# Sigmoid attention and a gated MLP on one core: SyncE's transfers in program order, the small sums as a step of their own, Q's part between two sigmoids

## The chip, the core and the metric

The kernel runs on one core of a Trainium2 chip. The core has five engines with a queue of instructions each: TensorE (PE, matrix products into PSUM; PEld is its loading of weights), VectorE (DVE), ScalarE (ACT), GpSimd (POOL), and SyncE (SP), which here only issues transfers. Each engine works through its queue in order and waits on semaphores for the others. The metric is the device time of one execution in microseconds (us), less is better.

## The reference

Eight batches of twelve heads, 448 tokens of 64 numbers each. Attention weighs with a sigmoid instead of a softmax; the heads are laid side by side into rows of 768, and an MLP follows whose gate is h - tanh(h).

```python
# q, k, v: (8, 12, 448, 64)   w_in: (768, 2048)   w_out: (2048, 768)
scores = q @ k.transpose(0, 1, 3, 2) / sqrt(64) - log(448)
x = (1 / (1 + exp(-scores))) @ v          # then (8 * 448, 768)
h = x @ w_in
out = (h - tanh(h)) @ w_out
```

Everything is float32 outside. Inside, a number is mostly split into two float16 parts, scaled by a power of two, and a product is made of three matmuls (high by high, high by low, low by high).

## The kernel before, in words

**Batches.** Batch 0 is computed in float32 (`attention32`, `moe1_32`), while both weight matrices are loaded, converted and split. From then on each batch b does two things: `moe1` (L748), the product with `w_in` with the gate computed by `mix` behind it, and `moe2` (L857), the product with `w_out`. The attention of batch b + 1 runs in small steps between the matmuls of `moe2` of batch b. Batch 1 keeps its attention weights in float32 (`AV32 = 2`); batches 2 to 7 split them.

**Positions.** `moe2` is a generator: it gives way after every six full-width matmuls (`po`, L876), 48 times, and then 16 times after six half-width ones (`por`, L914), which count half. A table (`BLOCKS`; `BLOCKS0` and `BLOCKS1` for batches 0 and 1) holds the positions at which the next step of the attention is taken from the generator `stream` (L451). So the order of each engine's queue is written out by hand.

**Steps.** `stream` goes by pairs of heads (g, h = g + 1), four steps each, which this document calls A to D. `sc` are scores in PSUM (L380), `a` their sigmoid on ACT (L391), `ahl` the two float16 parts of `a` (high on ACT L397, rest on DVE L398), `acc` the product of `ahl` with the parts `vhl` of v (L411), `x` the evacuated `acc` (L425 or L427).

- A: scores and sigmoids of g's row blocks 0 and 1; the products `acc` left over from the steps before; `ahl`; square sums of v (`sqn`, L317).
- B: scores and sigmoids of g's block 2 and of the half block that g and h share; square sums of k and q of head g + 3; `ahl`.
- C: `scales(g + 2)`, which is a tiny matmul `pbn` (L325) over the square sums, its evacuation `tn` on ACT (L327), and a chain of six tiny DVE instructions to the scales `sn` (L336); scores of h's blocks 0 and 1; its first sigmoid; K's part of head g + 2; its second sigmoid; the products `acc`; `vhl`; `ahl`; Q's part of g + 2; loads of head g + 4.
- D: scores and sigmoid of h's block 2; K's part, `ahl`, Q's part of head g + 3; square sums of head g + 4.

A "part" (`parts`, L345) turns a loaded k or q into two float16 halves `w` (first half L351 on ACT or L353 on DVE, second half L354 on DVE) and then transposes them by a DMA that SP issues (L356) into the tile K or Q, which the scores read. `w` has two buffers.

**Queues.** The whole program stands in a block that keeps PE, ACT, DVE and POOL in the order in which the code is written. SP isn't named there: its transfers are put in an order by the framework's scheduler.

**Square sums of x.** `add_squares` (L431) sums the squares of the six `x` tiles of a batch: two of the six squares are made on ACT (L437), the other four on POOL (L439), all sums on POOL (L448).

**Weights in batch 0.** While `moe2` of batch 0 runs, the pieces of `w_out` (`rawo`, L131, then `stb` on ACT L146 and DVE L151 to L155, and a small matmul `wl`, L179) are still converted, and `w_in` and `w_out` (`wi`, `wo`) are split on ACT (L216) and DVE (L219), at positions of their own between the steps.

Of the kernel before, what the change touches and what calls it, by code (L numbers as in the profile page):

```python
# [34 lines left out]
class Builder:  # L35
# [4 lines left out]
    SPLIT = 16, 0.78  # L40
    CONV = 0.95

    BLOCKS = (8, 11, 16, 20, 24, 27, 32, 36, 40, 43, 48, 52)
    TAIL = (1, 2, 3, 4, 5)
    ALONE = 9
    BLOCKS0 = (2, 5, 8, 12, 16, 20, 24, 31, 38)
    BLOCKS1 = (4, 7, 10, 13, 16, 20, 24, 27, 32, 36, 40, 43, 48, 52)

    TP = 8
    SHIFT = 4  # L50
# [368 lines left out]
    def evac_x(self, j, acc, iv):  # L419
        nc = self.nc  # L420
        x = self.xp.tile([P, self.S], F32, name="x32", tag="x")
        if iv is None and self.xs is None:
            nc.vector.tensor_copy(x, acc[:, : self.S])  # L423
        elif iv is None:
            nc.scalar.activation(x, acc[:, : self.S], AF.Copy)  # L425
        else:
            nc.scalar.activation(x, acc[:, : self.S], AF.Copy, scale=iv)  # L427
        self.add_squares(j, x)
        return x

    def add_squares(self, j, x):  # L431

        nc = self.nc
        last = j == self.NP - 1
        x2 = self.xp.tile([P, self.S], BF16 if last else F32, name="x2", tag="x2", bufs=2)
        if last or j == 0:
            nc.scalar.activation(x2, x, AF.Square)  # L437
        else:
            nc.gpsimd.tensor_tensor(x2, x, x, op=ALU.mult)  # L439
        if j == 0:  # L440
            self.x2 = x2
        elif last:
            self.x2b = self.x2, x2
        else:
            out = self.x2
            if j == self.NP - 2:
                out = self.xp.tile([P, self.S], BF16, name="x2b", tag="x2b", bufs=1)
            nc.gpsimd.tensor_tensor(out, self.x2, x2, op=ALU.add)  # L448
            self.x2 = out

    def stream(self):  # L451

        NP = self.NP
        G = (self.B - 1) * NP
        at = lambda g: (1 + g // NP, g % NP)
        splits = lambda g: at(g)[0] >= self.AV32
        qk, vn, sc, K, Q, vv, accs = {}, {}, {}, {}, {}, {}, {}  # L460

        def load(g):
            if g < G and g not in qk:
                qk[g] = self.load_qk(*at(g))

        def load_v(g):
            if g < G and splits(g):
                vn[g] = self.load_v(*at(g), self.nat, "vn", 2)

        def sums(g):  # L470
            ss = self.sums[g // 2 % 2]
            return ss if splits(g) else ss[:, :4]

        def norms(g):
            if g < G:
                for n, t in enumerate(qk[g]):
                    self.norm(t, sums(g)[:, 2 * n + g % 2 : 2 * n + g % 2 + 1])

        def norm_v(g):
            if g in vn:  # L480
                self.norm(vn[g], sums(g)[:, 4 + g % 2 : 5 + g % 2])

        def scales(g, where):
            if g < G:
                sc[g] = sc[g + 1] = self.scales(sums(g), where)

        def parts_k(g):
            if g < G:
                K[g] = self.parts(qk[g][0], sc[g][0][:, 0:1], "K", not splits(g) and g not in (2, 3))

        def parts_q(g):
            if g < G:
                Q[g] = self.parts(qk[g][1], sc[g][0][:, 1:2], "Q", True)
                qk.pop(g)

        def prep_v(g):
            if g >= G:
                return
            if splits(g):
                vv[g] = self.prep_v(vn.pop(g), sc[g][0])  # L500
            else:
                vv[g] = self.load_v(*at(g), self.att, "vhl", 3)[:, None]

        load(0)
        load(1)
        yield 0, False
        norms(0)
        norms(1)
        yield 0, False
        scales(0, "tr")  # L510
        parts_k(0)
        yield 450, False
        parts_q(0)
        load(2)
        yield 450, False
        parts_k(1)
        yield 450, False
        parts_q(1)
        load(3)
        yield 450, False  # L520
        norms(2)
        yield 0, False
        todo = []

        def open_acc(g):
            tag = "tr" if g % 2 else "av"
            accs[g] = self.ps.tile([P, 512], F32, name="acc", tag=tag, bufs=1)
            if g % NP == 0:
                self.xs = []

        def close_acc(g):
            iv = sc[g][1][:, 1:2] if splits(g) else None
            self.xs.append(self.evac_x(g % NP, accs.pop(g), iv))
            if g % 2:
                vv.pop(g - 1)
                vv.pop(g)
            for d in (sc, K, Q):
                d.pop(g)

        def do_av():  # L540
            for g, c, A in todo:
                odd = g % 2
                if c == QT:
                    open_acc(g + 1)
                    self.av([accs[g], accs[g + 1]], vv[g], A, c, odd)
                    close_acc(g)
                    continue
                if c == 0 and not odd:
                    open_acc(g)
                self.av([accs[g]], vv[g], A, c, odd)  # L550
                if c == QT - 1 and odd:
                    close_acc(g)
            todo.clear()

        def units(g, cs, between=lambda: None):

            pss = []
            for c in cs:
                n = 2 if c == QT else 1
                pss.append(self.scores([K[g + i] for i in range(n)], [Q[g + i] for i in range(n)], c))  # L560
            aa = [self.weigh(pss[0], sc[g][1][:, 0:1])]
            between()
            aa += [self.weigh(ps, sc[g][1][:, 0:1]) for ps in pss[1:]]
            return aa

        def keep(g, cs, aa):
            if splits(g):
                aa = [self.split_a(a) for a in aa]
            todo.extend((g, c, a) for c, a in zip(cs, aa))

        for g in range(0, G, 2):
            h = g + 1
            early = g == 0

            aa = units(g, (0, 1))
            do_av()
            if early:
                prep_v(0)
                prep_v(1)
            keep(g, (0, 1), aa)  # L580
            load(g + 3)
            norm_v(g + 2)
            norm_v(g + 3)
            yield 2750, True

            aa = units(g, (2, QT))
            if early:
                do_av()
            norms(g + 3)
            keep(g, (2, QT), aa)  # L590
            yield 2750, True

            scales(g + 2, "mm" if early else "av")
            aa = units(h, (0, 1), lambda: parts_k(g + 2))
            do_av()
            prep_v(g + 2)
            keep(h, (0, 1), aa)
            parts_q(g + 2)
            prep_v(g + 3)
            load(g + 4)  # L600
            load_v(g + 4)
            load_v(g + 5)
            yield 2750, True

            aa = units(h, (2,), lambda: parts_k(g + 3))
            if early:
                do_av()
            keep(h, (2,), aa)
            parts_q(g + 3)
            norms(g + 4)  # L610
            yield 2750, True
        do_av()
        yield 1150, True
# [314 lines left out]
    def build(self):  # L928
        nc, tc = self.nc, self.tc
# [19 lines left out]
        E = mybir.EngineType  # L949
        with tc.manual_schedule(engines={E.PE, E.Activation, E.DVE, E.Pool}):  # L950
# [5 lines left out]
            self.blocks = self.stream()  # L956
            self.moe1_32(self.xs, weights, rest)
            self.first(self.convert([(q, False) for q in pieces[nA + self.NF :]]))
            for b in range(1, self.B):
                self.batch(b)  # L960
        self.gp.release()

    def first(self, rest):

        n = 4
        next(self.tail)
        ahead = [self.split_w_out(0)]
        for k in range(n):
            next(self.blocks)
            for _ in range(2):  # L970
                next(self.tail, None)
            if k == 1:
                next(ahead[0])
            if k == 2:
                self.finish_g()
                next(ahead[0])
# [1 line left out]
        next(rest)  # L978
        next(ahead[0])
        next(rest)  # L980
        assert n + len(self.BLOCKS0) + len(self.BLOCKS1) == 4 * self.NP + len(self.BLOCKS) - self.ALONE
        split = self.split_w_in()
        at, each = self.SPLIT
        events = [(at + k * each, lambda: next(split, None)) for k in range(self.NC * self.NB + 1)]
# [7 lines left out]
            ahead[0] = self.split_w_out(1)  # L992

        events += [(at, scale)] + [(at + 0.5 * k, lambda: next(ahead[0], None)) for k in range(1, self.NF // 2 + 1)]
        self.second(0, self.BLOCKS0, 2 * self.NP - n, events)

    def batch(self, b):

# [69 lines left out]
```

## Time and profile before

| what | value |
| --- | --- |
| runs shown | 1250.58 us median of 3 (1249.23 to 1251.46) |
| the profiled execution, its own time | 1250.92 us |
| its span, first to last instruction | 1249.1 us |
| mean granted clock of PE | 0.982 |
| q1 (SP's transfers) | 88.28 MB, 31.1% of 16 DMA engines' span |

A row of the timeline gives the start in us, the duration in us, the engine, the line in the kernel, the operation with its tiles (written `out<-in`), the shape, how many in a row, and in brackets how long the engine stood idle before it and what released it. A row of the waits gives the waiting engine and tile, what it waited for, the total in us, how often, and the longest. A row of the table by stretches gives, for each engine, the busy time and the number of instructions, then PE's granted clock as a share of full speed, the busy share of the DMA engines, and GB/s.

### The profile page before, as it was taken

What the parts mean: (1) busy time and instruction counts of PE and PEld (TensorE: products, weight loads), DVE (VectorE), ACT (ScalarE), POOL (GpSimd) and SP (SyncE); (2) the same over time, 40 slices, a digit from 0 to 9 for tenths busy, and PEclk for the clock granted to TensorE, in tenths of its full rate; (3) what the DMA queues carried; (4) which work ended last, traced back from release to release, by engine and by line L of the source; (5) the groups of instructions that cost most, each with busy time, mean ns of one, the idle gap of its engine ahead of it and who ended that gap; (6) DMA issues with size and microseconds to landing.
All of it is one profiled execution on the core that took longest, in us unless ns stands there. A gap on an engine that the chain in (4) does not pass through costs nothing.

```text
span 1249.1 us, 19741 instructions
## 1 busy us (share of the span) xinstructions
PE 1183.5 (95%) x7633; PEld 612.2 (49%) x7633; DVE 932.9 (75%) x1376; ACT 884.6 (71%) x1230; POOL 87.3 (7%) x70
## 2 busy tenths in 40 slices
PE   8889976699989999999999999999999999999998
PEld 3235423255545555555555555545555555555555
DVE  5889977867975789767985789757985789736930
ACT  5657775865887768776888768776888768754820
POOL 0200001000002000110001000110001000110000
PEclk9899979799999999999999999999999999999999
DMA  9973448230034420253014420354014420310000
GB/s 227 257 209 83 90 89 216 57 87 14 1 73 101 87 51 1 66 113 89 1 30 100 87 52 1 70 116 82 1 30 100 87 52 1 58 29 20 1 13 33
DMA packets 225679, 89.78 MB, mean 72 GB/s; under 512 B 213936, under 2 KB 215728, under 8 KB 225584
## 3 DMA queue, kind: packets, MB, share of 16 engines
q1 hardware_dynamic: 224656, 88.28, 31.1%
q8 instruction: 60, 0.98, 0.3%
q10 hardware_dynamic: 928, 0.23, 0.1%
q14 instruction: 35, 0.29, 0.1%
HBM read 58.20 MB, written 11.01 MB: 55 GB/s over the span
## 4 chain that ended last, share of the span: by engine, by line
PE 65%; DVE 13%; ACT 10%; issue 6%; DMA 5%; SPq 1%; DVEq 0%; ACTq 0%
PE ph L761 30%; PE po L876 17%; PE acc L411 6%; PE por L914 5%; PE sc L380 5%; DMA Q<-w 3%; DVE ahl L398 3%; ACT ahl L397 3%; ACT a L391 2%; ACT sqn L317 2%; DVE sta L152 1%; DMA rawo<-moe_w_out 1%; DVE w L354 1%; DVE m L835 1%; DVE m L846 1%
## 5 line engine op out<-in xcount | busy, mean ns | idle before, releaser
L876 PE MATMUL po<-wo,g 128*128 128x384 f16 x2304 | 393.4, 327 | 4.6 <-DVE wo L219 2.0
L761 PE MATMUL ph<-xhl,wi 128*128 128x448 f16 x2016 | 382.6, 352 | 0.0
L876 PEld LDWEIGHTS <-g 128*128 128x128 f16 x2304 | 219.5, 98 | 179.5 <-issue 39.0
L761 PEld LDWEIGHTS <-wi 128*128 128x128 f16 x2016 | 196.7, 98 | 185.0 <-issue 1.8
L398 DVE SCALAR_TENSOR_TENSOR ahl<-a,ahl 128x896 f16<-128x896 f32 x126 | 156.9, 1279 | 137.3 <-ACT ahl L397 137.3
L391 ACT ACTIVATE a<-sc,nls,rn 128x896 f32<-128x896 f32 x147 | 154.4, 1090 | 40.8 <-PE sc L380 36.8
L831 ACT ACTIVATE u<-ph,ih 128x896 f32<-128x896 f32 x64 | 64.4, 1006 | 98.2 <-PE ph L761 93.5
L380 PE MATMUL sc<-Q,K 64*128 64x448 f16 x1008 | 104.6, 362 | 17.3 <-DMA Q<-w 12.3
L397 ACT ACTIVATE ahl<-a 128x896 f16<-128x896 f32 x126 | 113.2, 941 | 0.6
L439 POOL TENSOR_TENSOR x<-x 128x448 f32<-128x448 f32 x32 | 30.9, 965 | 1023.3 <-ACT x L427 788.5
L835 DVE SCALAR_TENSOR_TENSOR m<-ph,ihk,u 128x896 f32<-128x896 f32 x64 | 73.5, 1149 | 32.0 <-ACT th L833 31.6
L745 ACT ACTIVATE g<-m,Sg 128x896 f16<-128x896 f32 x64 | 66.7, 1041 | 34.4 <-DVE m L849 29.0
L411 PE MATMUL acc<-ahl,vhl 128*64 128x448 f16 (+1 forms) x864 | 82.0, 359 | 1.1 <-ACT tn L327 1.1
L849 DVE COPY_PREDICATED m<-u,th 128x896 f32<-128x896 uint32 x64 | 77.3, 1207 | 6.6
L746 DVE SCALAR_TENSOR_TENSOR g<-m,Sg,g 128x896 f16<-128x896 f32 x64 | 73.4, 1146 | 6.7 <-ACT g L745 6.7
L846 DVE SCALAR_TENSOR_TENSOR m<-q,m 128x896 f32<-128x896 f32 x64 | 69.9, 1092 | 10.9 <-ACT q L845 3.9
L791 PE MATMUL ph<-x,wi 128*128 128x448 f32 x192 | 76.1, 545 | 1.6 <-DVE x L423 1.6
L380 PEld LDWEIGHTS <-K 64*128 64x128 f16 x1008 | 37.7, 98 | 76.4 <-issue 54.9
L836 DVE SCALAR_TENSOR_TENSOR th<-ph,ih,th 128x896 f32<-128x896 f32 x64 | 73.3, 1145 | 0.0
L848 ACT ACTIVATE u<-u,b 128x896 f32<-128x896 f32 x64 | 66.8, 1043 | 8.0 <-DVE m L835 6.2
L842 DVE SCALAR_TENSOR_TENSOR m<-q,m 128x896 f32<-128x896 f32 x64 | 69.5, 1086 | 0.0
L914 PE MATMUL por<-wo,g 128*64 128x384 f16 x768 | 64.9, 327 | 1.1 <-ACT o L905 1.1
(133 smaller groups left out, 1204.1 us busy)
## 6 DMA issues: line engine op xcount, KB each, us to landing
raw<-moe_w_in SPq DMA_DIRECT2D x24, 512.0 KB, 5.1
rawo<-moe_w_out SPq DMA_DIRECT2D x32, 384.0 KB, 4.3
kn<-k SPq DMA_DIRECT2D x96, 112.0 KB, 2.9
qn<-q SPq DMA_DIRECT2D x94, 112.0 KB, 2.9
vn<-v SPq DMA_DIRECT2D x96, 96.0 KB, 2.6
out<-o SPq DMA_DIRECT2D x21, 384.0 KB, 2.4
vn<-v SPq DMA_DIRECT2D x48, 32.0 KB, 2.3
out<-orem SPq DMA_DIRECT2D x16, 96.0 KB, 2.2
```

Source lines behind the costliest of these rows:

```text
L380: self.nc.tensor.matmul(ps[i * m : (i + 1) * m, h, : self.S], K[i][r, w, c * P : c * P + m], Q[i][r, x, :], start=(n == 0), stop=(n == len ...
L391: self.nc.scalar.activation(a[:, 0], ps[:, :, : self.S], AF.Sigmoid, bias=self.nls, scale=scale)
L397: nc.scalar.activation(A[:, 0], a[:, 0], AF.Copy, scale=A_SCALE)
L398: nc.vector.scalar_tensor_tensor(A[:, 1], a[:, 0], A_SCALE, A[:, 0], op0=ALU.mult, op1=ALU.subtract)
L411: self.nc.tensor.matmul(acc[i][h * D : (h + 1) * D, : self.S], v[k, w, 2 * QT + h if half else h * QT + c], A[k, x, h], start=(n == 0 and ...
L761: nc.tensor.matmul(ph[:, e, :S], self.wi[:, c * self.NB + k, part, e * P : (e + 1) * P], xhl[c][:, x, :], start=(i == 0), stop=(i == 3 * s ...
L791: nc.tensor.matmul(ph[:, e, :S], self.where("in", c)[:, f * P : (f + 1) * P], xs[c], start=(c == 0), stop=(c == self.NC - 1),)
L835: V.scalar_tensor_tensor(m, ps, ihk, u, op0=ALU.mult, op1=ALU.mult)
L846: V.scalar_tensor_tensor(m, q2, C2, m, op0=ALU.add, op1=ALU.mult)
L849: V.copy_predicated(m, u.bitcast(U32), th)
L876: nc.tensor.matmul(po[i][:, :H], gs[f // 2][:, x, f % 2, tk * P : (tk + 1) * P], self.wo[:, i * self.NF + f, w], start=(f == 0 and n == 0) ...
L914: nc.tensor.matmul(po[e * D : (e + 1) * D, :H], gs[f // 2][:, x, f % 2, nm:S], self.wo[:, e * self.NF + f, w], start=(f == 0 and n == 0), ...
```

## The change

Five things change.

1. From batch 1 on SP is named too: its transfers stand in the order in which the code is written.
2. The tiny matmul, its evacuation, the scale chain and K's part of head g + 2 leave step C and become a step S of their own, which yields. The tables get one position for each S, two before that of its C (20 becomes 18 and 20), or one before it (8 of `BLOCKS0` and 7 of `BLOCKS1`).
3. Q's part of head g + 2 moves from the end of step C to between its two sigmoids, where K's part was.
4. In batches 0 and 1 (where `x` is evacuated without a scale, `iv is None`) the four squares that were POOL's go to ACT.
5. `first`, `second` and `ALONE` count the new steps.

```diff
-    BLOCKS = (8, 11, 16, 20, 24, 27, 32, 36, 40, 43, 48, 52)
+    BLOCKS = (8, 11, 16, 18, 20, 24, 27, 32, 34, 36, 40, 43, 48, 50, 52)
-    ALONE = 9
-    BLOCKS0 = (2, 5, 8, 12, 16, 20, 24, 31, 38)
-    BLOCKS1 = (4, 7, 10, 13, 16, 20, 24, 27, 32, 36, 40, 43, 48, 52)
+    ALONE = 11
+    BLOCKS0 = (2, 5, 7, 8, 12, 16, 20, 22, 24, 31, 38)
+    BLOCKS1 = (4, 6, 7, 10, 13, 16, 18, 20, 24, 27, 32, 34, 36, 40, 43, 48, 50, 52)
...
-        self.add_squares(j, x)
+        self.add_squares(j, x, iv is not None)
...
-        if last or j == 0:
+        if last or j == 0 or not pool:
             nc.scalar.activation(x2, x, AF.Square)
         else:
             nc.gpsimd.tensor_tensor(x2, x, x, op=ALU.mult)
...
             scales(g + 2, "mm" if early else "av")
-            aa = units(h, (0, 1), lambda: parts_k(g + 2))
+            parts_k(g + 2)
+            yield 0, False
+
+            aa = units(h, (0, 1), lambda: parts_q(g + 2))
             do_av()
             prep_v(g + 2)
             keep(h, (0, 1), aa)
-            parts_q(g + 2)
             prep_v(g + 3)
...
+        with tc.manual_schedule(engines={E.PE, E.Activation, E.DVE, E.Pool, E.SP}):
             for b in range(1, self.B):
                 self.batch(b)
...
-        n = 4
+        n = 5
-        for k in range(n):
+        for k in range(n - 1):
+            if k == 2:
+                next(self.blocks)
             next(self.blocks)
```

What this does to the queues shows at three places. The first is PE in `moe2` of batch 2, between a step B and the step C behind it. Before, the tiny matmul stood right ahead of C's scores:

```order
L876 LDWEIGHTS g
L876 MATMUL po_4913<-wo,g 128x384
L325 MATMUL pbn<-ss_112,onesf 128x6
L380 LDWEIGHTS K
L380 MATMUL sc<-Q,K 128x448
```

Now it stands in the middle of the `po` matmuls (line 876 has become 878):

```order
L878 LDWEIGHTS g
L878 MATMUL po_4916<-wo,g 128x384
L325 MATMUL pbn<-ss_112,onesf 128x6
L878 LDWEIGHTS g
L878 MATMUL po_4915<-wo,g 128x384
```

There are 24 `po` matmuls between B's scores and C's; `pbn` had all 24 ahead of it and now has 12 ahead and 12 behind. Where the half-width `por` stand there (position 50), it is 24 and 24 of 48.

The second place is ACT in the same step C (names with numbers are the tiles of single sigmoids and evacuations). Before:

```order
L327 ACTIVATE tn<-pbn,tiny 128x6
L391 ACTIVATE a_4967<-sc,nls,rn 128x896
L391 ACTIVATE a_4974<-sc,nls,rn 128x896
L427 ACTIVATE x_5008<-acc,rn 128x448
L397 ACTIVATE ahl<-a_4967 128x896
L397 ACTIVATE ahl<-a_4974 128x896
L351 ACTIVATE w<-qn,sn 112x512
L391 ACTIVATE a_5075<-sc,nls,rn 128x896
```

Now:

```order
L327 ACTIVATE tn<-pbn,tiny 128x6
L391 ACTIVATE a_4975<-sc,nls,rn 128x896
L351 ACTIVATE w<-qn,sn 112x512
L391 ACTIVATE a_4982<-sc,nls,rn 128x896
L427 ACTIVATE x_5016<-acc,rn 128x448
L397 ACTIVATE ahl<-a_4975 128x896
L397 ACTIVATE ahl<-a_4982 128x896
L391 ACTIVATE a_5078<-sc,nls,rn 128x896
```

The first half of Q's part has moved ahead of four instructions; `tn` has the same neighbours ahead of it as before. On DVE the second half of Q's part (L354) moves in the same way, ahead of one `vhl` pair and two `ahl`, to right behind K's.

The third place is ACT in `moe2` of batch 0, from the square sums of the step B at position 20 to the first sigmoid of the step C at 24, where the splits of `wo` and `wi` stand between the steps. Before:

```order
L317 ACTIVATE sqn,ss_114<-qn 112x512
L216 ACTIVATE wo<-wo,swo_s 128x384 x2
L216 ACTIVATE wi<-wi,swi_s 128x256
L216 ACTIVATE wo<-wo,swo_s 128x384 x2
L216 ACTIVATE wi<-wi,swi_s 128x256
L216 ACTIVATE wo<-wo,swo_s 128x384 x4
L216 ACTIVATE wi<-wi,swi_s 128x256
L216 ACTIVATE wo<-wo,swo_s 128x384 x4
L895 ACTIVATE oh<-po,iK 128x384
L216 ACTIVATE wi<-wi,swi_s 128x256 x2
L327 ACTIVATE tn<-pbn,tiny 128x6
L391 ACTIVATE a_2040<-sc,nls,rn 128x896
```

Now, from the second split of `wi` on:

```order
L216 ACTIVATE wi<-wi,swi_s 128x256
L216 ACTIVATE wo<-wo,swo_s 128x384 x4
L327 ACTIVATE tn<-pbn,tiny 128x6
L216 ACTIVATE wi<-wi,swi_s 128x256
L216 ACTIVATE wo<-wo,swo_s 128x384 x4
L897 ACTIVATE oh<-po,iK 128x384
L216 ACTIVATE wi<-wi,swi_s 128x256 x2
L391 ACTIVATE a_2045<-sc,nls,rn 128x896
L351 ACTIVATE w<-qn,sn 112x512
```

`tn` has moved ahead of seven splits and one evacuation. On SP, from batch 1 on, each step's K and Q transposes now stand next to each other, ahead of the loads that are written behind them; before, loads of k and v stood between the two. In batch 0 the scheduler has ordered SP anew as well: the transposes of the step C at 8 and the loads of five `rawo` pieces behind them have the same transfers ahead of them, in another order.

More of the change, by code (lines that the diff above doesn't have):

```diff
@@ L427, in evac_x, with add_squares @@
             nc.scalar.activation(x, acc[:, : self.S], AF.Copy, scale=iv)
-        self.add_squares(j, x)
+        self.add_squares(j, x, iv is not None)
         return x
-    def add_squares(self, j, x):
+    def add_squares(self, j, x, pool):
         nc = self.nc
@@ L980, in first @@
         next(rest)
-        assert n + len(self.BLOCKS0) + len(self.BLOCKS1) == 4 * self.NP + len(self.BLOCKS) - self.ALONE
+        assert n + len(self.BLOCKS0) + len(self.BLOCKS1) == 5 * self.NP + len(self.BLOCKS) - self.ALONE
         split = self.split_w_in()
@@ L994, in first @@
         events += [(at, scale)] + [(at + 0.5 * k, lambda: next(ahead[0], None)) for k in range(1, self.NF // 2 + 1)]
-        self.second(0, self.BLOCKS0, 2 * self.NP - n, events)
+        self.second(0, self.BLOCKS0, len(self.BLOCKS0) - 1, events)
     def batch(self, b):
```

## The prediction

> **What bounds the kernel now.** I read the page's totals first, then PE's table by stretches, then PE's waits, then the timeline at the places where the longest waits stand.
>
> ```profile
> span 1249.1 us, 19741 instructions
> PE 1183.5 (95%) x7633; PEld 612.2 (49%) x7633; DVE 932.9 (75%) x1376; ACT 884.6 (71%) x1230; POOL 87.3 (7%) x70
> 150.00:250.00 100.00, 69.27 (x392) 28.82 (x392) 78.02 (x158) 73.43 (x131) 7.60 (x6) 0.86 0.51 120
> 250.00:344.00 94.00, 94.00 (x578) 49.91 (x575) 74.83 (x116) 66.96 (x100) 2.72 (x2) 0.99 0.15 34
> ...
> 440.00:1125.00 685.00, 677.42 (x4688) 360.05 (x4683) 526.61 (x714) 520.06 (x690) 55.88 (x40) 1.00 0.27 55
> ```
>
> PE is busy 1183.5 of 1249.1 us, so the 65.6 us in which it stands idle are all that a new order can win. They lie unevenly: 30.7 us in the hundred from 150 to 250 (the first steps of batch 1's attention, with `moe2` of batch 0), and only 7.6 us in the 685 from 440 to 1125. From 250 to 344 PE is never idle: what it gains ahead of 250 it keeps. PE's longest waits that the change can touch, over the span, then from 440 to 1200 and from 150 to 290:
>
> ```profile
> PE sc L380 <- DMA Q<-w: 12.3, 13, 2.1
> PE acc L411 <- ACT tn L327: 9.4, 3, 7.1
> ...
> PE sc L380 <- DMA Q<-w: 7.4, 9, 1.2
> ...
> PE sc L380 <- DMA Q<-w: 1.2, 1, 1.2
> ```
>
> **The wait for Q.** The timeline of the first pair in `moe2` of batch 3, from step B to the next pair's step A:
>
> ```profile
> 655.37 1.43 PE L380 MATMUL sc<-Q,K 64*128 64x448 f16 x18
> 656.16 2.09 ACT L391 ACTIVATE a<-sc,nls,rn 128x896 f32<-128x896 f32 x2 [0.26 <-PE sc L380]
> 656.74 4.07 PE L876 MATMUL po<-wo,g 128*128 128x384 f16 x24
> 659.27 0.20 ACT L317 ACTIVATION_READ_ACCUMULATOR sqn<-qn 112x1 f32 x1
> 660.65 0.28 PE L325 MATMUL pbn<-ss,onesf 128*128 128x6 f32 x2
> 660.86 1.31 PE L380 MATMUL sc<-Q,K 64*128 64x448 f16 x12
> 661.04 0.26 ACT L327 ACTIVATE tn<-pbn,tiny 128x6 f32<-128x6 f32 x1
> 662.94 0.18 DVE L336 RECIPROCAL sn<-in 128x3 f32<-128x3 f32 x1
> 663.67 0.75 DVE L354 SCALAR_TENSOR_TENSOR w<-kn,sn,w 112x512 f16<-112x512 f32 x1
> 666.23 3.09 DVE L398 SCALAR_TENSOR_TENSOR ahl<-a,ahl 128x896 f16<-128x896 f32 x2 [0.62 <-ACT ahl L397]
> 666.93 0.71 ACT L351 ACTIVATE w<-qn,sn 112x512 f16<-112x512 f32 x1
> 669.24 0.74 DVE L354 SCALAR_TENSOR_TENSOR w<-qn,sn,w 112x512 f16<-112x512 f32 x1
> 670.01 1.25 SPq L356 DMA_TRANSPOSE Q<-w  x1
> 673.13 1.31 PE L380 MATMUL sc<-Q,K 64*128 64x448 f16 x12 [0.73 <-DMA Q<-w]
> ```
>
> Q's second half ran on DVE at 669.24, behind two `ahl` of 3.09 us; SP issued the transpose 0.03 us after it ended (669.98, 670.01) and it took 3.1 us until PE went on. So it was Q's place on ACT and DVE, not SP's order, that held A back. After the change ACT makes the first half behind the first sigmoid, and DVE the second right behind K's, which ends at 664.42: it ends near 665.2, SP issues it behind K's transpose near 666, and it lands near 669, more than 3 us before A. SP's program order by itself is worth nothing here; it only keeps Q's transpose from standing behind loads of v that wait for `vhl`. Twelve of the 13 waits lie behind such a step C (the one of 1.2 us, in batch 0, does not shorten, since `sn` comes late there): **-11.1 us** (12.3 - 1.2). What is late next is `tn`, and DVE's queue, which does the same work in another order.
>
> **The new wait at pbn.** `pbn` needs the square sums of q, which ended at 659.47 (659.27 + 0.20). PE passed the twelfth of the 24 `po` at 656.74 + half of 4.07, so at 658.77; by the single start times of the trace, in which the last end is modelled, at 658.70. It will stand for 0.76 us plus some 0.05 of signalling. ACT can't be earlier: it stood idle for 0.26 us before the sigmoids until PE's scores were there. And nobody gains: `tn` started at 661.04, behind ACT's `ahl`, and its place there does not change. In `moe2` of batches 2 to 6 there are three such places in each of four and one in the last, 13 x 0.81 = 10.5 us. In batch 1 the positions 18, 34 and 50 find ACT in another state; between nothing and 0.81 each I take half, 1.2 us. Position 6 of batch 1 trades a longer wait at `pbn` for a wait of `acc` on `tn`: nothing. Sum **+11.7 us**, bounds 10.5 and 12.9. Of the steady part nothing is left: +0.6.
>
> **Batch 0, the step C at 24.** Here ACT had a pile of splits ahead of `tn`, and `acc` waits for `tn`, since both use one PSUM bank:
>
> ```profile
> 238.24 0.39 PE L325 MATMUL pbn<-ss,onesf 128*128 128x6 f32 x2 [1.48 <-ACT sqn L317]
> 240.90 2.12 ACT L216 ACTIVATE wo<-wo,swo_s 128x384 f16<-128x384 f32 x4
> 246.60 0.26 ACT L327 ACTIVATE tn<-pbn,tiny 128x6 f32<-128x6 f32 x1
> 246.92 5.77 PE L411 MATMUL acc<-a,vn 128*64 128x448 f32 x20 [7.05 <-ACT tn L327]
> ```
>
> Now `tn` comes right behind those four `wo`, at 243.0, and ends at 243.3. PE waits at `pbn` until 238.24 as before (3.5 instead of 1.48 us, two groups of `po` being behind it now: 12 x 0.17 = 2.0), then does these two groups and C's scores (1.3), arrives at 241.8 and goes on at 243.3: **-3.7 us** against 246.92, kept to the end by the full stretch behind it.
>
> What a long wait also costs shows beside the same 20 matmuls at the step C at 8:
>
> ```profile
> 202.29 3.39 PE L411 MATMUL acc<-a,vn 128*64 128x448 f32 x20 [1.21 <-ACT tn L327]
> ```
>
> They took 3.39 us behind 1.21 us of idling, 5.77 behind 7.05, and the granted clock of the stretch was 0.86. The Trainium skill, "TensorE: Matmul & The Clock Gate", section "What's actually happening", has PE's clock halved after an idle window of about 3.4 us, until it has been busy for as long. By this the 3.5 us at `pbn` would slow the twelve `po` and the scores behind it; the trace agrees that idling slows what follows, and which of the two waits does it here no row can tell. My sum has neither a gain nor a loss for it.
>
> **Batch 0, the step C at 8.** `pbn` moves ahead of one group of `po`, and `w_out`'s pieces get other places in SP's queue:
>
> ```profile
> 199.46 0.39 PE L325 MATMUL pbn<-ss,onesf 128*128 128x4 f32 x2 [1.24 <-ACT sqn L317]
> 212.54 2.40 SPq L131 DMA_DIRECT2D rawo<-moe_w_out  x5
> 216.66 0.55 ACT L146 ACTIVATE stb<-rawo 128x384 f32<-128x384 f32 x1 [6.63 <-DMA rawo<-moe_w_out]
> 221.17 0.48 PE L179 MATMUL wl<-stb,onesb 128*128 128x384 bf16 x1 [5.61 <-DVE stb L152]
> ```
>
> PE waits for `sqn` until 199.46 either way, then has 1.0 us of `po`, a `wl` and 1.3 of scores ahead of `acc`: 202.5 instead of 202.29, +0.2. On ACT, `tn` goes ahead of `oh` and one `stb`, and Q's first half ahead of the second sigmoid and one `x`: a sigmoid (1.05) and three short instructions of some 0.55 each, as the `stb` above, are 2.7 us. By so much Q's transpose, and the five pieces behind it in SP's queue, can be issued earlier (212.54 down to 209.8), and with them the 5.61 us wait shrinks. Between nothing and 2.7 (a buffer may hold the pieces back) I take half: **-1.4 + 0.2 us**.
>
> **The squares.** Eight squares leave POOL for ACT. In batch 0's attention DVE is the chain, and it is slowed while POOL runs:
>
> ```profile
> 56.45 0.91 DVE L151 TENSOR_SCALAR sta<-sta 128x512 uint32<-128x512 uint32 x1
> 59.55 0.42 DVE L151 TENSOR_SCALAR sta<-sta 128x512 uint32<-128x512 uint32 x1
> 67.86 1.15 DVE L151 TENSOR_SCALAR sta<-sta 128x512 uint32<-128x512 uint32 x1
> L437 ACT ACTIVATE x<-x 128x448 f32<-128x448 f32 (+1 forms) x16 | 9.2, 577 | 2.0 <-DVE x L423 1.1
> ```
>
> The same instruction takes 0.42 us alone, 0.91 and 1.15 beside a square on POOL: 0.5 + 0.7 = 1.2 us off DVE's chain. ACT gets 8 x 0.577 = 4.6 us, beside which it stands waiting for DVE there. I take **-1.2 us**, bounds -2.4 (all four squares alike) and +4.6 (nothing hidden).
>
> **Sum.** -11.1 + 11.7 - 3.7 - 1.4 + 0.2 - 1.2 = -5.5 us. Against the profiled execution's 1250.92 that is 1245.4; it lay 0.3 us above the median of the runs, so I say 1245.1.
>
> **Rivals.**
>
> *More comes back, because the clock stays up.* If the shorter waits in batch 0 leave the clock full, `acc` at C takes 3.39 and not 5.77 us (-2.4), and all of the 2.7 is had (-1.3): 1241.4. For it speaks that 1.21 us of idling cost nothing there; against it, that 3.5 us are still waited at once. Chance 0.18.
>
> *Nothing is left.* The early gains fail (the clock's rule takes up to the doubled 2.0 + 1.3 = 3.3 of the 3.7; the pieces are held back; ACT's squares eat what DVE gains), and the steady part is +0.6: about 1251. Chance 0.28.
>
> *Slower: ACT stands at Q's part.* It is queued ahead of the second sigmoid and needs `sn`. That costs nothing while `sn` is there within a sigmoid (1.05 us) of the first one's start; with C's scores 0.85 later in the steady part that holds (sigmoid from about 662.4, `sn` at 663.1). In batch 0 DVE is behind:
>
> ```profile
> 169.02 0.24 ACT L327 ACTIVATE tn<-pbn,tiny 128x4 f32<-128x4 f32 x1
> 171.96 0.17 DVE L336 RECIPROCAL sn<-in 128x2 f32<-128x2 f32 x1
> ```
>
> The first sigmoid ends about 1 us behind `tn`, near 170.2, `sn` at 172.1: ACT stands for 1.9 us. ACT's splits of `wo`, for which `po` waits, are queued behind it. At C of 8 K's half is ACT's too; I price it the same. With the four squares' 2.3 us in batch 1 on the same queue that is 6.1 us, and with no early gain 1251.5 + 6.1 = 1257.6. Chance 0.12; I gave it nothing in the sum, since a load of q levels the first of these out:
>
> ```profile
> 182.78 0.63 ACT L317 ACTIVATE sqn<-qn 112x512 bf16<-112x512 f32 x1 [2.33 <-DMA qn<-q]
> ```
>
> *The change does not do what it says:* it does, the order of the queues shows it; only that SP's order is what mattered is ruled out above.
>
> **How the numbers follow.** The forecast, 1243 to 1248, has 0.42. The range of eight in ten takes in the better clock down to 1240 and the bounds of `pbn`, squares and pieces up to 1252.5. A measurement can tell about 0.2%, 2.5 us: faster than 1248.1 are the forecast and the better clock, 0.60; within it 0.28; above 1253.1 the slower rival, 0.12.
>
> **What would show it.** Right: after 340 no wait of PE for Q, and some 13 waits of about 0.8 us for `sqn` at `pbn`, so PE's idle time from 440 to 1125 stays near 8 to 9 us; `acc` at C of 24 waits for 1.5 us instead of 7.05, `wl` for less than 5.61. Wrong: waits for Q that remain, waits at `acc` for `ahl` in A, a longer stretch from 150 to 250, or a PE that gives way at `pbn` without a loss.

## The result, and the profile after

| what | before | after |
| --- | --- | --- |
| median of the runs | 1249.90 us (1248.34 to 1251.46, 4 runs) | 1240.82 us (1240.29 to 1243.69, 4 runs) |
| the profiled execution, its own time | 1250.92 us | 1240.89 us |
| mean granted clock of PE | 0.982 | 0.988 |

The ratio of after to before is 0.9932, with a 95% interval of 0.9912 to 0.9952: faster by 0.5 to 0.9%. The forecast was 1245.1 us; the range from 1240.0 to 1252.5 holds the result, near its lower end. It lies below the forecast's own 1243 to 1248, beside the first rival (1241.4).

The totals of the page of the changed kernel, and its table by stretches (busy us and instructions of PE, PEld, DVE, ACT, POOL, then the granted clock, the DMA share and GB/s):

```profile
span 1239.1 us, 19719 instructions
PE 1182.8 (95%) x7633; PEld 606.5 (49%) x7633; DVE 927.8 (75%) x1376; ACT 887.6 (72%) x1238; POOL 77.7 (6%) x62
150.00:250.00 100.00, 76.81 (x447) 32.19 (x446) 75.94 (x160) 75.61 (x139) 4.55 (x4) 0.90 0.52 125
250.00:344.00 94.00, 92.12 (x576) 49.25 (x576) 80.02 (x120) 74.25 (x107) 0.00 (x0) 0.99 0.10 24
440.00:1125.00 685.00, 676.09 (x4710) 357.44 (x4709) 524.26 (x713) 513.10 (x682) 55.89 (x40) 1.00 0.25 54
```

PE does the same work in the same busy time (1183.5 before, 1182.8 now), so nearly all of the gain is idle time: 65.6 us before, 1239.1 - 1182.8 = 56.3 now. From 150 to 250 PE is busy for 76.8 instead of 69.3 us, and its granted clock is 0.90 instead of 0.86. From 440 to 1125 nothing is gained (676.1 and 677.4).

PE's waits at `pbn` in the kernel before over the span, then some of PE's waits in the changed kernel over the span, then its waits at `pbn` from 440 to 1125:

```profile
PE pbn L325 <- ACT sqn L317: 3.7, 3, 1.5
...
PE pbn L325 <- ACT sqn L317: 17.5, 18, 3.2
PE wl L179 <- DVE stb L152: 9.1, 8, 3.3
...
PE acc L411 <- ACT a L391: 2.8, 2, 2.0
...
PE pbn L325 <- ACT sqn L317: 8.4, 13, 0.7
```

No wait for Q is left, and no wait of `acc` for `tn`. In their place stand 18 waits at `pbn` (3 before), 13 of them from 440 on, of 8.4 / 13 = 0.65 us each.

Where the time was won shows in the start of the same matmuls in both traces:

| matmul | start before, us | after, us | difference |
| --- | --- | --- | --- |
| the third `wl`, in `moe1_32` | 86.21 | 82.28 | -3.9 |
| `pbn` of the step C at 24, batch 0 | 238.24 | 233.09 | -5.2 |
| first `por` in `moe2` of batch 0 | 281.04 | 269.98 | -11.1 |
| first `por` in `moe2` of batch 1 | 429.30 | 414.95 | -14.4 |
| end of the span | 1249.1 | 1239.1 | -10.0 |

By the first `por` of batch 1 14.4 us are won; what follows gives 4.4 of them back.

### The profile page after: what moved, and what is told of

Read it like the earlier page. It is cut to its first block, busy times and chain, and to the rows that moved or that the text cites. A ratio compares the mean times of both kernels' runs of the same rounds, so it can differ in the third digit from the quotient of the medians.

```text
span 1239.1 us, 19719 instructions
## 1 busy us (share of the span) xinstructions
PE 1182.8 (95%) x7633; PEld 606.5 (49%) x7633; DVE 927.8 (75%) x1376; ACT 887.6 (72%) x1238; POOL 77.7 (6%) x62
## 4 chain that ended last, share of the span: by engine, by line
PE 77%; DVE 8%; ACT 8%; issue 3%; DMA 3%; SPq 1%; ACTq 0%; DVEq 0%
PE ph L763 30%; PE po L878 27%; PE acc L411 8%; PE sc L380 7%; PE por L916 4%; ACT a L391 3%; ACT sqn L317 2%; DMA raw<-moe_w_in 1%; DMA qn<-q 1%; DVE m L837 1%; DVE m L848 1%; DVE sta L152 1%; DVE m L851 1%; DVE m L844 1%; DVE g L748 1%
## 5 line engine op out<-in xcount | busy, mean ns | idle before, releaser
L878 PE MATMUL po<-wo,g 128*128 128x384 f16 x2304 | 397.4, 328 | 6.2 <-ACT wo L216 3.1
L439 POOL TENSOR_TENSOR x<-x 128x448 f32<-128x448 f32 x24 | 22.4, 932 | 786.3 <-ACT x L427 786.3
```

What stands on the lines that cost most here:

```text
L878: nc.tensor.matmul(po[i][:, :H], gs[f // 2][:, x, f % 2, tk * P : (tk + 1) * P], self.wo[:, i * self.NF + f, w], start=(f == 0 and n == 0) ...
```

## The experiments

The times are medians. The kernel before ran beside every set of them, and its own medians there lie between 1249.19 and 1249.89 us (11 to 23 runs); ratios are to those.

### S one position later

```diff
-    BLOCKS = (8, 11, 16, 18, 20, 24, 27, 32, 34, 36, 40, 43, 48, 50, 52)
+    BLOCKS = (8, 11, 16, 19, 20, 24, 27, 32, 35, 36, 40, 43, 48, 51, 52)
...
-    BLOCKS1 = (4, 6, 7, 10, 13, 16, 18, 20, 24, 27, 32, 34, 36, 40, 43, 48, 50, 52)
+    BLOCKS1 = (4, 6, 7, 10, 13, 16, 19, 20, 24, 27, 32, 35, 36, 40, 43, 48, 51, 52)
```

> The changed kernel with S one position later from batch 1 on (18, 34, 50 become 19, 35, 51): pbn then has 18 instead of 12 po ahead of it, 1.02 us more, and waits 0.65 in the changed kernel. If that wait is the price of S, as my theory has it, the 13 waits of 0.65 us (8.5 us) in batches 2 to 6 and those of batch 1 (1.88 + 0.65 + 0.65, of which 1.0 at most each) go, and nothing takes their place, since tn on ACT stands behind ahl until about 0.4 us after pbn anyway: 1240.8 - 8.5 - 2.3 = 1230.0. Rival: the wait only moves on, since a later pbn makes tn and sn later and ACT then stands at Q's part or acc waits for tn: about 1240.8. PE's idle time from 440 to 1125 tells them apart: near 0.5 us or near 9.

Measured: 1227.89 us, ratio to before 0.9829 (0.981 to 0.9848). That is 12.9 us under the changed kernel. PE in `moe2` of batch 2, from the scores of B to `acc` in C (timeline; first the changed kernel, then this one):

```profile
502.03 1.43 PE L380 MATMUL sc<-Q,K 64*128 64x448 f16 x18
503.40 2.12 PE L878 MATMUL po<-wo,g 128*128 128x384 f16 x12
506.17 0.39 PE L325 MATMUL pbn<-ss,onesf 128*128 128x6 f32 x2 [0.65 <-ACT sqn L317]
506.42 2.11 PE L878 MATMUL po<-wo,g 128*128 128x384 f16 x12
508.46 1.31 PE L380 MATMUL sc<-Q,K 64*128 64x448 f16 x12
509.70 2.58 PE L411 MATMUL acc<-ahl,vhl 128*64 128x448 f16 x30
...
499.62 1.43 PE L380 MATMUL sc<-Q,K 64*128 64x448 f16 x18
500.99 3.10 PE L878 MATMUL po<-wo,g 128*128 128x384 f16 x18
503.93 0.28 PE L325 MATMUL pbn<-ss,onesf 128*128 128x6 f32 x2
504.07 1.14 PE L878 MATMUL po<-wo,g 128*128 128x384 f16 x6
505.13 1.31 PE L380 MATMUL sc<-Q,K 64*128 64x448 f16 x12
506.37 2.58 PE L411 MATMUL acc<-ahl,vhl 128*64 128x448 f16 x30
```

With 18 `po` ahead of it, `pbn` waits for nothing, and nothing else becomes late: `acc` comes 6.75 us behind B's scores instead of 7.67. PE's idle time from 440 to 1125 falls to 0.5 us (busy 684.49 of 685). The wait showed as 0.65 us, and its removal is worth 0.92 here. Most of the rest is overlap that a wait takes away: the 18 `po` start every (503.93 - 500.99) / 18 = 0.163 us, while a group of 12 ends by its row 0.16 us later than 12 such steps. The pair of `pbn` adds 0.11 (0.25 instead of 0.14 us to the next `po`). Over batches 2 to 6 `acc` of the last step C gains 13.5 - 2.4 = 11.1 us on that of batch 1's last, 0.85 us for each of 13 places. The rival falls.

Moving S on in batches 0 and 1 too, on top of this:

```diff
-    BLOCKS0 = (2, 5, 7, 8, 12, 16, 20, 22, 24, 31, 38)
+    BLOCKS0 = (2, 5, 7, 8, 12, 16, 20, 23, 24, 31, 38)
-    BLOCKS1 = (4, 6, 7, 10, ...
+    BLOCKS1 = (4, 7, 7, 10, ...
```

> The kernel with S one position later (1227.9), and S one later as well in batch 0 (22 becomes 23) and at the first place of batch 1 (6 becomes 7, right ahead of its C). The waits of 3.2 and 1.9 us at pbn shrink by one group of po, 1.02 us each, if nothing takes their place: 1227.9 - 2.0 = 1225.9. Rival: tn comes later by as much, and acc then waits for it: 1228.

Measured: 1232.10 us, ratio 0.9865 (0.9847 to 0.9884), 4.2 us slower than with the one edit above. `acc` waits for `tn` again, 3.2 us at the step C at 24 and 1.1 in batch 1: the rival (1228) was right in kind, and short in size. The waits are longer than what was saved at `pbn`, and behind the one of 3.2 us the 20 matmuls of `acc` take 5.02 instead of 3.39 us. Later is better only as long as `tn` isn't what comes last.

### Q's place, and SP's order

Four kernels: the changed one with Q's part back at the end of C, the same with SP left to the scheduler, the changed one with SP alone left to the scheduler, and the kernel before with SP in program order.

```diff
-            aa = units(h, (0, 1), lambda: parts_q(g + 2))
+            aa = units(h, (0, 1))
...
             keep(h, (0, 1), aa)
+            parts_q(g + 2)
```

> The changed kernel with Q's part back at the end of step C, S kept, SP kept in program order. Theory (Q's place on ACT and DVE caused the waits for Q): the 12 waits of about 0.9 us come back, 1240.8 + 11.1 = 1252, PE's idle time from 440 to 1125 near 16 us. Rival (SP's program order is what removed them): 1241, no wait of PE for Q.

> The changed kernel with Q's part back at the end of C and SP in the scheduler's order; S is kept. If the extra 14.6 us of the run with Q behind came from SP's program order: 1240.8 + 11.1 = 1251.9, with 12 or more waits of about 0.9 us for Q. If S itself (K's part earlier) made them: 1266.

```diff
-        with tc.manual_schedule(engines={E.PE, E.Activation, E.DVE, E.Pool, E.SP}):
-            for b in range(1, self.B):
-                self.batch(b)
+            for b in range(1, self.B):
+                self.batch(b)
```

> The changed kernel with SP's transfers again in the scheduler's order, all else kept. Theory (SP's order is worth nothing by itself): 1240.8 within 1 us, no waits of PE for Q behind step C. Rival (it keeps Q's transposes from standing behind loads that wait for a buffer, and is needed): waits for Q of about 1 us at 12 places or more, 1252.

> The kernel before with SP in program order from batch 1 on and nothing else. The prediction held that SP's order by itself is worth nothing: 1249.3. With S kept and Q's part at the end of C it cost more than the waits for Q can explain (1266.5 against 1240.8 + 11.1 = 1251.9), and SP stood 100 us ahead of transposes behind loads of v that wait for vhl. If that comes from the order of SP and not from S, this kernel takes about 1249.3 + 14.6 = 1264.

| Q's part of C | SP from batch 1 on | with S | without S (the kernel before) |
| --- | --- | --- | --- |
| behind C | scheduler | 1250.74 | 1249.9 |
| behind C | program order | 1266.51 | 1268.99 |
| between the sigmoids | scheduler | 1240.11 | |
| between the sigmoids | program order | 1240.82 | |

With SP free, Q's place is worth 1250.74 - 1240.11 = 10.6 us, and the waits for Q come back with it (10.1 us in 13). With Q's part between the sigmoids SP's order is worth nothing: 1240.11 and 1240.82, within their spread. With Q's part behind C, SP's program order costs 15.8 us, and on the kernel before 19.1. So the first of these runs, at 1266.51, met neither of its expectations (1252 and 1241). From 440 to 1125, waits of SP that the view puts down to `vhl`, of ACT's square sums for loads, and of PE, first before, then before with SP in program order:

```profile
SPq L356 <- DVE vhl L367: 14.6, 7, 5.2
ACT sqn L317 <- DMA qn<-q: 2.6, 7, 0.6
...
SPq L356 <- DVE vhl L367: 65.5, 14, 5.8
ACT sqn L317 <- DMA kn<-k: 8.3, 8, 1.2
PE sc L380 <- DMA Q<-w: 8.6, 12, 1.1
PE nm L688 <- ACT x L437: 3.7, 4, 1.8
```

The waits of SP have grown from 14.6 to 65.5 us. What they are for shows in the rows of SP and DVE behind a step C: first the kernel before, then the changed one with Q's part behind C and SP in program order:

```profile
664.48 1.25 SPq L356 DMA_TRANSPOSE K<-w  x1
665.79 1.14 SPq L287 DMA_DIRECT2D kn<-k  x2
...
692.10 1.22 SPq L356 DMA_TRANSPOSE K<-w  x1
692.46 0.75 DVE L367 SCALAR_TENSOR_TENSOR vhl<-vn,sn,vhl 128x512 f16<-128x512 f32 x1
697.78 0.74 DVE L354 SCALAR_TENSOR_TENSOR w<-qn,sn,w 112x512 f16<-112x512 f32 x1
698.55 1.22 SPq L356 DMA_TRANSPOSE Q<-w  x1
699.83 1.13 SPq L287 DMA_DIRECT2D kn<-k  x2
699.94 0.75 DVE L354 SCALAR_TENSOR_TENSOR w<-kn,sn,w 112x512 f16<-112x512 f32 x1
706.34 1.25 SPq L356 DMA_TRANSPOSE K<-w  x1
```

SP stands not for the `vhl` ahead of it, which ends at 693.2, but at Q's transpose, which needs the second half of Q's part: that ends at 698.52, and SP issues 0.03 us later. In program order the loads of the next k, q and v stand behind this transpose; the scheduler had put the load of k ahead of it, at 665.79, and Q's transpose at 670.01. The next transpose of K, whose operand is there at 700.69, then stands behind these loads until 706.34. ACT's square sums wait for the loads, and ACT is then late for `x` and PE's tiny matmuls over it (`nm`). With Q's part between the sigmoids the operand of Q's transpose is there before SP has issued K's (in `moe2` of batch 2 at 511.75 and 512.37 us), and Q's follows at 512.46, so nothing stands behind it; that fits with the same order being free there. How the 15.8 and 19.1 us divide over this chain wasn't separated.

### Batch 0, the step C at 24

S put right ahead of its C, all else as in the changed kernel; and then the same with PE kept busy during the wait by 26 matmuls whose results the next scores overwrite.

```diff
-    BLOCKS0 = (2, 5, 7, 8, 12, 16, 20, 22, 24, 31, 38)
+    BLOCKS0 = (2, 5, 7, 8, 12, 16, 20, 24, 24, 31, 38)
```

> The changed kernel with one position changed: in batch 0, S goes from 22 to 24, right ahead of its C, so tn stands behind the seven splits and the evacuation again. The prediction's term for this place was 3.7; by PE's start times behind and ahead of it, it was 5.9. So 1240.8 + 5.9 = 1246.7 by the traces, 1244.5 by the prediction's term, with acc waiting 5 to 7 us for tn. Rival (the gain there came from SP's order or from Q's place): 1241 with a short wait of acc.

```diff
         ps = self.ps.tile([P, 2, 512], F32, name="sc", tag="sc", bufs=2)
+        for _ in range(fill):
+            w = self.onesb[:, None, :].to_broadcast([P, 4, P])
+            self.nc.tensor.matmul(ps[:, 0, :], self.onesb, w, start=True, stop=True)
...
+                fill = 26 if g == 5 and c == 1 else 0
```

> The kernel with S of batch 0 at 24 (1246.9), where PE stands 7.05 us ahead of acc and the 20 matmuls of acc then take 5.52 us instead of 3.39. 26 matmuls of 128x512 whose results are overwritten stand between the two score tiles of that step C: PE works through them while it would wait for tn, and arrives at acc with a wait of 1 to 1.5 us. If the 2.1 us more of acc are what idling costs (the term that the prediction put at nothing), acc takes 3.39 us and the time is 1246.9 - 2.1 = 1244.8. If acc is slow there for another reason (ACT or DVE beside it), it stays at 5.5 us and the time at 1246.9, or above it if the added matmuls last longer than the wait.

Measured: 1246.90 us (ratio 0.9975, 0.9966 to 0.9983) and 1244.58 (0.9968, 0.9954 to 0.9982). PE there, in the changed kernel, with S at 24, and with PE kept busy:

```profile
233.09 0.39 PE L325 MATMUL pbn<-ss,onesf 128*128 128x6 f32 x2 [3.23 <-ACT sqn L317]
233.34 3.69 PE L878 MATMUL po<-wo,g 128*128 128x384 f16 x12
236.96 1.36 PE L380 MATMUL sc<-Q,K 64*128 64x448 f16 x12
238.25 3.39 PE L411 MATMUL acc<-a,vn 128*64 128x448 f32 x20
...
231.94 0.39 PE L325 MATMUL pbn<-ss,onesf 128*128 128x6 f32 x2 [1.98 <-ACT sqn L317]
232.26 1.31 PE L380 MATMUL sc<-Q,K 64*128 64x448 f16 x12
240.62 5.52 PE L411 MATMUL acc<-a,vn 128*64 128x448 f32 x20 [7.05 <-ACT tn L327]
...
232.65 0.74 PE L383 MATMUL sc<-Q,K 64*128 64x448 f16 x6
233.32 5.79 PE L376 MATMUL sc<-onesb 128*128 128x512 bf16 x26
239.04 0.74 PE L383 MATMUL sc<-Q,K 64*128 64x448 f16 x6
241.01 3.39 PE L414 MATMUL acc<-a,vn 128*64 128x448 f32 x20 [1.23 <-ACT tn L327]
```

The place is worth 1246.90 - 1240.82 = 6.1 us. The same 20 matmuls of `acc` take 5.52 us behind 7.05 us of idling and 3.39 where PE worked until 1.2 us ahead of them; ACT and DVE do the same work beside both. The 2.3 us that the median gains (1246.90 to 1244.58) are `acc`'s 2.1 within the spread, though PE did 5.8 us more work. So the slowness is the price of idling itself. PE's granted clock in the same traces says by what means:

| stretch, us | what PE does | granted clock |
| --- | --- | --- |
| S at 24, 236.0 to 240.6 | stands | 0.50 |
| S at 24, 240.6 to 246.0 | `acc` | 0.60 |
| PE kept busy, 236.0 to 241.0 | the added matmuls, scores, 1.23 us of wait | 1.00 |
| PE kept busy, 241.0 to 244.4 | `acc` | 1.00 |
| changed kernel, 233.0 to 237.0 | `pbn`, the 12 `po` | 0.59 |
| changed kernel, 238.2 to 241.6 | `acc` | 1.00 |

In the changed kernel the price has moved: its 12 `po` behind 3.23 us at `pbn` take 3.69 instead of 2.12 us, and `acc` has the full clock again.

### The squares

On the kernel before, the eight squares moved to ACT and nothing else; and, on the kernel with S later, those of batch 1 put back on POOL.

```diff
-        if last or j == 0:
+        if last or j == 0 or not pool:
```

> The kernel before with the eight squares moved from POOL to ACT and nothing else. The prediction's term was -1.2 us. In the changed kernel the first wait for stb stands 3.9 us earlier than before; if the squares did that alone and it is kept, this kernel takes 1249.9 - 3.9 = 1246.0; by the prediction's term 1248.7; if the 3.9 came from SP's new order in batch 0 or another edit, 1250 and the first wait for stb stays at 86.2.

```diff
-        self.add_squares(j, x, iv is not None)
+        self.add_squares(j, x, self.xs is not None)
```

> The kernel with S one position later (1227.9), with the four squares of batch 1's x back on POOL; those of batch 0 stay on ACT. If all of the squares' gain is in batch 0's attention, and ACT has room in moe2 of batch 0: 1227.9. If batch 1's squares stand on ACT's path to the splits of wo: up to 4 x 0.58 = 2.3 us less, 1225.6. If POOL's squares slow DVE on the path there too: slower by up to 2.

Measured: 1246.35 us (0.9979, 0.9966 to 0.9993), 3.0 less than before, and 1228.88 (against 1227.89 with all squares on ACT, within the spread). So the gain, or all but some 1 us of it, is in batch 0's attention. Three steps of PE in `moe1_32` (timeline), before and with the squares moved, and in the latter the two instructions of DVE that the prediction counted (0.91 and 1.15 us there):

```profile
75.45 1.02 PE L791 MATMUL ph<-x,wi 128*128 128x448 f32 x2 [1.60 <-DVE x L423]
79.19 5.68 PE L791 MATMUL ph<-x,wi 128*128 128x448 f32 x12
84.71 0.27 PE L247 MATMUL pt<-ident,st 128*1 128x128 f32 x1
...
73.65 1.02 PE L791 MATMUL ph<-x,wi 128*128 128x448 f32 x2 [0.25 <-DVE x L423]
76.86 4.67 PE L791 MATMUL ph<-x,wi 128*128 128x448 f32 x12
81.37 0.27 PE L247 MATMUL pt<-ident,st 128*1 128x128 f32 x1
...
55.87 0.42 DVE L151 TENSOR_SCALAR sta<-sta 128x512 uint32<-128x512 uint32 x1
66.79 0.42 DVE L151 TENSOR_SCALAR sta<-sta 128x512 uint32<-128x512 uint32 x1
```

The two instructions of DVE are 1.2 us shorter, as forecast. DVE delivers `x` earlier, PE gets to the first row 1.8 us sooner, and idles for 0.25 instead of 1.60 us ahead of it. From there to the twelve `ph` it takes 0.5 us less, and these take 4.67 instead of 5.68 us: 84.71 - 81.37 = 3.3 us at the last row. The last 1.5 us of them are again PE's speed behind a wait: its granted clock is 0.85 from 75 to 79 and 0.81 from 79.0 to 84.7 before, and 1.00 in both steps with the squares moved.

### Two more places of batch 0

S of batch 0 at 8, right ahead of its C, in place of 7:

```diff
-    BLOCKS0 = (2, 5, 7, 8, 12, ...
+    BLOCKS0 = (2, 5, 8, 8, 12, ...
```

> The changed kernel (1240.8) with S of batch 0 at 8, right ahead of its C, in place of 7. The prediction had -1.4 + 0.2 = -1.2 us for this place, and PE's starts show -1.3 from pbn there to the next C: 1242.0, with the wait of wl for stb at 5 us instead of 3.25. Rival: the wait of 2.7 us at pbn and the slow po and scores behind it go with the place, which gives back as much: 1240.8.

Measured: 1242.38 us (0.9952, 0.9939 to 0.9966), 1.6 more than the changed kernel (0.9932, 0.9912 to 0.9952); the two overlap, so the difference isn't clear of the spread. The profile is one of its two longest executions (six from 1240.96 to 1245.69), and shows what can make them differ. `pbn` and `acc` in it, and behind them the wait for `stb`:

```profile
195.15 0.39 PE L325 MATMUL pbn<-ss,onesf 128*128 128x4 f32 x2 [1.24 <-ACT sqn L317]
195.47 1.31 PE L380 MATMUL sc<-Q,K 64*128 64x448 f16 x12
198.08 6.30 PE L411 MATMUL acc<-a,vn 128*64 128x448 f32 x20 [1.31 <-ACT tn L327]
220.14 0.48 PE L179 MATMUL wl<-stb,onesb 128*128 128x384 bf16 x1 [4.31 <-DVE stb L152]
```

The kernel before had the same two waits, 1.24 and 1.21 us, and `acc` took 3.39 us behind them, here 6.30. The granted clock was 1.00 there from 199.4 to 205.6; here it is 0.50 from 198 to 201 and 0.53 from there to 204.3. The 1.6 us agree with the term in size; how much of them is the wait for `stb` (4.31 instead of 3.25) and how much such chance, one profile can't say. The term is neither confirmed nor refuted.

Q's part of the first pair back at the end of C, on the kernel with S later:

```diff
-            aa = units(h, (0, 1), lambda: parts_q(g + 2))
+            aa = units(h, (0, 1), lambda: None if early else parts_q(g + 2))
...
+            if early:
+                parts_q(g + 2)
```

> The kernel with S one position later (1227.9), with Q's part of the first pair alone (the steps in moe1_32 and the first positions of moe2 of batch 0) back at the end of C. The slower rival's mechanism, ACT standing at Q's part until sn is there, shows in the changed kernel as acc waiting 1.98 us for a sigmoid at 170.0, and its wo splits behind it as a wait of 2.71 us of po. If it costs what these waits show, 1227.9 - 1.7 = 1226.2, less the waits for Q of 1 to 2 us that come back; if the wait for sqn levels it out, as the prediction held, 1227.9.

Measured: 1227.59 us, against 1227.89: no difference. PE's wait of 1.98 us for the sigmoid goes, and others grow: the next one for DVE's split of `wo` is 1.39 instead of 0.89 us, and one of 0.55 for Q comes back. The start of the next `wl`, which waits for `stb`, is the same within 0.1 us: 184.91, against 185.00.

## Why the prediction was right, and where it was short

| term of the sum | predicted | what the runs show |
| --- | --- | --- |
| waits for Q | -11.1 | -10.6 (Q's place, SP free) |
| wait at `pbn` | +11.7 | +12.9 (S one position later takes it away) |
| C at 24 | -3.7 | -6.1 (S at 24) |
| C at 8 | -1.4 + 0.2 | -1.6 (S at 8), not clear of the spread |
| squares | -1.2 | -3.0 (squares alone) |
| sum | -5.5 | -8.4, against -9.1 measured between the medians |

**Waits for Q and at pbn: right.** The two nearly cancel, as forecast, and the steady part loses a little. The price of a place, 0.81 us, was read from B's `sqn` and the twelfth `po`. Its rows show 0.65 and its removal gives 0.85; the forecast comes nearer to that than the rows, since it went by the start times of the `po`. In batch 1 the wait at position 6 was put at nothing, and stood for 1.9 us there, but `acc` no longer waits for `tn`.

**C at 24: the mechanism right, the size short.** `acc` was forecast to start 3.6 us earlier (243.3 against 246.92), and it starts at 238.25, on the clock of the kernel before (5.15 later) at 243.40. The way there differs: the 1.5 us of waiting for `tn` did not come, since the `po` behind the 3.23 us wait were slow by 1.57 us, and the scores behind them no longer (1.36 us). The rule of the Trainium skill that the prediction cites ("TensorE: Matmul & The Clock Gate", section "What's actually happening") gives the full clock back after about 3.4 us of work. The trace agrees: the `po` at half speed lasted 3.69 us, and the scores behind them had a granted clock of 0.96; that both would be slowed, as the prediction put it, went too far. What was missed is what lies behind: the 20 matmuls of `acc` fell from 5.77 to 3.39 us. The step that failed is the sentence "My sum has neither a gain nor a loss for it": there were both, and the gain of 2.4 was on the path to the end, while the loss took the place of a wait. The first rival had it, and with that term the sum comes to -7.9. It had it by another road, a clock that stays full (0.59 at the `po`), and its second half, the rest of the pieces at C of 8, isn't shown; what brought the result near its 1241.4 besides is the squares, worth 1.8 us more than it had for them. That agreement is partly luck.

**Squares: the mechanism right, the size short.** The term counted two instructions of DVE that were slowed (1.2 us). Those are shorter by just that. The 3.3 us at the last row hold 1.5 us more by which PE's next steps run faster when it idles less, the same omission, and 0.6 us by which DVE was ahead already; the whole kernel keeps 3.0.

**SP's order.** "SP's program order by itself is worth nothing here" holds where the change made it; as a statement on SP alone it was wrong: on the kernel before it costs 19 us, and Q's part had to move for it to be free. The reason given, loads of v that wait for `vhl`, was wrong too: in program order it is the loads that stand behind Q's transpose.

**The rivals.** "ACT stands at Q's part" happens, as a wait of 1.98 us at `acc`, and costs nothing. With Q's part behind C ACT is 2.9 us ahead at its splits of `wo` (169.05 against 171.91) and only 0.5 us behind its waits for the loads of k and q (177.91 against 178.45): these level it out, as the prediction argued. "Nothing is left" fell with the early gains, which were larger than thought. The range was wide enough to the low side only because it took in the first rival.

**The better version.** The forecast priced the wait at `pbn` as given by the position 18. That `tn` has nothing to lose there ("its place there does not change") also meant that `pbn` could come one group later for free; with it the kernel takes 1227.89 us, 0.983 of the time before.

## What to carry to other kernels

A small matmul that must stand early for the engines behind it has a window: not before its operand, not after its reader is free. Read both ends from the trace and put it at the late end; one group of six matmuls at each place was worth 12.9 us over the kernel. Price a wait of PE by more than its row: here 0.65 us shown cost 0.85, and idling of some three microseconds took the granted clock down to 0.59 for the matmuls behind it. A queue in program order stands at its latest operand: make that operand early before fixing the order.

## What the hardware showed that was not expected

- PE's speed behind idling, by the rows above: twelve scores took 1.31 us behind 1.98 us of idling, as they do where PE doesn't wait; twelve `po` took 3.69 instead of 2.12 behind 3.23; `acc` took 5.52 instead of 3.39 behind 7.05. But shorter waits can do it too, in one execution and not in another. `acc` also took 6.30 us behind waits of 1.24 and 1.31 with work between, where the same waits had cost nothing in the kernel before. And in batch 0, where the changed kernel and the one with S one position later run the same code, 18 scores behind the same wait of 1.43 us took 2.50 us in the one (185.80, granted clock 0.54) and 1.43 in the other (185.26, clock 1.00); a longer wait five microseconds ahead of that was 2.71 us in the one and 2.11 in the other. The Trainium skill, "TensorE: Matmul & The Clock Gate", section "What's actually happening", has the gate watch a window of about 3.4 us that runs on by itself, so that where in it the work falls decides. The chance in these cases agrees with it. That a full idle window is needed does not agree: 1.24 and 1.31 us of idling, apart from each other, were enough, and the measurement decides.
- Work on PE that is thrown away made the kernel faster: 26 matmuls of 5.8 us, put into a wait, took 2.3 us off the time.
